# A decode block on one core: the last fourteenth of w2 moved to GpSimd's DMA queue

## The chip, the cores and the metric

The kernel runs on one core of a Trainium2 chip. The core has five engines that run beside each other: TensorE (PE), VectorE (DVE), ScalarE (ACT), GpSimd (POOL) and SyncE (SP). Loads from HBM to SBUF are issued by one of them and carried out by sixteen load engines. The metric is the time of one execution on the device, in microseconds (us). A time quoted as a result is the median of several runs; the profile shows one further execution.

## The reference, cut to what matters

The output is the sum of the input `x`, grouped-query attention over a cache, and a dense layer with Mish, both on the layer-normalised `x`. There are 8 batches with one query each, D = 512, 32 query heads over 8 key heads, 8192 cached positions of 128 values, and F = 1792 hidden values.

```python
xn = _layernorm(x, axis=-1)
return x + _A_ref(xn, A_k_cache, A_v_cache, A_wq, A_wo) + _B_ref(xn, B_w1, B_b1, B_w2)

# _A_ref
q = (x @ wq).reshape(B, Sq, Hq, Dh).transpose(0, 2, 1, 3)
scores = jnp.einsum("bhqd,bhkd->bhqk", q, k) * (Dh ** -0.5)
o = jnp.einsum("bhqk,bhkd->bhqd", _softmax(scores), v)
return o.transpose(0, 2, 1, 3).reshape(B, Sq, Hq * Dh) @ wo

# _B_ref
h = jnp.einsum("bsd,df->bsf", x, w1) + b1
return jnp.einsum("bsf,fd->bsd", mish(h), w2)
```

All data are float32. The caches are nearly all of the 561 MB that each execution reads.

## The kernel before, in words

**Loop.** The work is cut into sixteen packs of two batches and two key heads. For each pack and each of its two batches, 8 MB of keys (`kT`) and 8 MB of values (`v`) come into two big buffers, `kva` and `kvb`. PE forms the scores into the PSUM banks `c0` and `c1` (`scores`), gathers them into `s` (`rows`), DVE and ACT form the weights `pt`, and PE sums the values into `o0` and `o1` (`values`). DVE folds these into `os` (`gather`), PE sums over partitions into `m` (`merge`), and DVE scales them into `oT` (`collect`). At the end of four packs `turn` and `outputs` multiply by a part of `wo`. The Mish half runs once at the start (`mish`); its result, transposed, stays in `aT` until the end of the kernel.

**Order.** A small recording layer (`Program`) keeps the operations of each engine in the order of the code and works out which semaphores each must wait for. An engine runs its operations in that order, so whatever stands behind a waiting operation waits too. All large loads are issued by SP on one queue, in the order of the list `queue`; a load is issued when its buffer is free (`release`, `pump`). Since every recorded operation is issued by one helper, the profile gives nearly all of them the same line (L383), and they are told apart by the names of their tiles.

**End.** After the last pack the code writes out: the sum of the values of the first batch (`values(0)`, from `kvb`), the sums of the weights (`sums`, `over`), two rounds of products whose result nobody reads (`unread(2)`, on `sc` and `ones`, into `c`), `merge(0)`, then `add_up`, which starts the last accumulation in `h` from the four groups of rows of `acc` (`acc` holds `x` and the earlier parts of `wo`), `unread(2)` again, the values of the second batch from `kva` (two loads, `va` with three quarters and `vb` with the last), `gather(1)`, `merge(1)`, `collect(1)`, `turn`. Then come the products of `w2` (`down`) and of the last part of `wo` (`last_outputs`) in five pieces, as they land: 8 of 14 rows of w2, three quarters of wo, 5 rows, the last quarter of wo, 1 row. A "row" of w2 is a block of 128 partitions by 512 columns (256 KB). DVE copies `h` out and SP stores it.

The five pieces go into `kvb`, whose first half is free once `values(0)` has read it; SP waits for a signal of that (`read`), and issues them behind the two loads of the second batch's values.

A product with weights of 8 or 32 columns fills a quarter of PE's columns; four such products to different rows of a bank run beside each other. In the profile, one float32 product is two records.

Of the kernel before, what the change touches and what calls it, by code (L numbers as in the profile page):

```python
# [1 line left out]

# [10 lines left out]
P = 128  # L13
B = 8
D = 512
# [7 lines left out]
G = 4  # L23
# [8 lines left out]
Q = P // G  # L32
# [27 lines left out]
W2R = G * FT // 2 * FP // P  # L60
# [4 lines left out]
LOOPED = ("tensor", "vector", "scalar")  # L65
FIRST, END = 1, PACKS
RARE = ("w",)
SOMETIMES = {
    "turn": lambda p: (p + 27) & 19,
    "queries": lambda p: (p + 1) & 19,  # L70
# [39 lines left out]
class Program:  # L110
# [43 lines left out]

    @staticmethod
    def region(ap):
        (step, n), *free = ap.ap
        p, f = divmod(ap.offset, step)
        return p, p + n, f, f + 1 + sum(s * (c - 1) for s, c in free)

    def conflicts(self, op):

# [281 lines left out]
def kernel(  # L444
# [13 lines left out]
    prog = Program(nc)  # L458
    pe, dve, act, pool, sp = (getattr(prog, e) for e in ("tensor", "vector", "scalar", "gpsimd", "sync"))

    def tile_of(shape, name):
        prog.on_chip.add(name)
        return nc.alloc_sbuf_tensor(name, list(shape), F32).ap()
# [8 lines left out]
    acc = tile_of([P, D], "acc")  # L472
    qc = tile_of([P, B, KR, REP], "qc")
    aT = tile_of([P, 2 * W2R, Q], "aT")
# [8 lines left out]
    def rows_of(blocks):  # L483

        return blocks.rearrange("j p f -> (j p f)").rearrange("(p f) -> p f", p=P)
# [13 lines left out]
    def release(what, relay=None):  # L499

        at = next(at for at, w in taken.items() if w == what)
        del taken[at]
        if relay:
            held[at] = [relay]
        pump()
# [57 lines left out]
    plan_v(PACKS - 1, 0, "b", "v0", lo=KX * BW)  # L563
    plan_v(PACKS - 1, 1, "a", "va", (0, 3 / 4))
    plan_v(PACKS - 1, 1, "a", "vb", (3 / 4, 1))
    W2_PARTS = ((0, 8), (8, 13), (13, 14))
    WO_PARTS = ((0, 3), (3, 4))
    for k, (lo, hi) in enumerate(W2_PARTS):
        plan("w2", "b", w2, ("w2a", "w2b", "w2c")[k], (lo / (2 * W2R), hi / (2 * W2R)))
# [7 lines left out]
    H = bank([P, 512], "h")  # L577
# [42 lines left out]
    os = [tile_of([P, DH], f"os{b}") for b in range(PB)]  # L620
    oT = tile_of([P, 2, REP, B], "oT")
    oW = tile_of([P, OR, 2, B], "oW")

    def setup():
        pool.memset(ident, 0.0)
        pool.affine_select(
            out=ident,
            in_=ident,
            compare_op=ALU.not_equal,
            fill=1.0,  # L630
            base=0,
            pattern=[[-1, P]],
            channel_multiplier=1,
        )
        pool.memset(ones, 1.0)
        dve.memset(xnT, 0.0)
        dve.memset(O[1], 0.0)
        dve.memset(os[1], 0.0)
        dve.memset(rt, 0.0)
        dve.memset(M[:, 168 : 168 + PB * 2 * REP], 0.0)  # L640

        st = tile_of([B, 8], "st")

        scratch = pt.rearrange("p b c m t e h -> p (b c m t e h)")
        xc, sq = scratch[:B, :D], scratch[:B, D : 2 * D]
        dve.reduce_sum(st[:, 0:1], x_sb, axis=AX.X)
        dve.tensor_scalar_mul(st[:, 1:2], st[:, 0:1], 1.0 / D)
        dve.tensor_scalar(xc, x_sb, st[:, 1:2], None, op0=ALU.subtract)
        dve.tensor_mul(sq, xc, xc)
        dve.reduce_sum(st[:, 2:3], sq, axis=AX.X)  # L650
        dve.tensor_scalar(
            st[:, 3:4], st[:, 2:3], 1.0 / D, EPS, op0=ALU.mult, op1=ALU.add
        )
        act.activation(st[:, 4:5], st[:, 3:4], AF.Sqrt)
        dve.reciprocal(st[:, 5:6], st[:, 4:5])

        dve.tensor_mul(st[:, 6:7], st[:, 5:6], st[:, 5:6])
        dve.tensor_mul(st[:, 7:8], st[:, 6:7], st[:, 3:4])
        dve.tensor_scalar(st[:, 6:7], st[:, 7:8], -0.5, 1.5, op0=ALU.mult, op1=ALU.add)
        dve.tensor_mul(st[:, 4:5], st[:, 6:7], st[:, 5:6])  # L660
        dve.tensor_scalar(xc, xc, st[:, 4:5], None, op0=ALU.mult)
        xr = wide[:B, : QR * P]
        pool.tensor_copy(
            xr.rearrange("b (r i s) -> b r i s", r=QR, i=PAIRS),
            xc.rearrange("b (o s r) -> b r o s", o=1, r=QR).to_broadcast([B, QR, PAIRS, P // PAIRS]),
        )
        for r in range(QR):
            pe.transpose(M[:, r * B : (r + 1) * B], xr[:, r * P : (r + 1) * P], ident[:B, :B])
        for i in range(PAIRS):
            rows = slice(Q * i, Q * (i + 1))  # L670
            act.copy(
                xnT[rows, :, :, B * i : B * (i + 1)],
                M[rows, : QR * B]
                .rearrange("p (r o b) -> p r o b", r=QR, o=1)
                .to_broadcast([Q, QR, 2, B]),
            )

        xs = scratch[:B, 2 * D : 2 * D + W1R * P]
        for t in range(2):
            pool.tensor_copy(  # L680
                xs.rearrange("b (r c t i) -> b r c t i", r=W1R, c=CC, t=2)[:, :, :, t, :],
                xc.rearrange("b (c i r) -> b r c i", c=CC, r=W1R),
            )

        dve.tensor_copy(
            gsel, ident[:G, :G].rearrange("p (g o) -> p g o", o=1).to_broadcast([G, G, B])
        )
        dve.reduce_sum(bsel, ident.rearrange("p (u i) -> p u i", u=KN), axis=AX.X)
        dve.reduce_sum(
            half, ident.rearrange("p (g t i) -> p t g i", g=G, t=2), axis=AX.XY  # L690
        )
        dve.reduce_sum(rsel, ident.rearrange("p (g r) -> p r g", g=G), axis=AX.X)
        dve.reduce_sum(hsel, rsel.rearrange("p (i r) -> p r i", i=W4), axis=AX.X)
        dve.reduce_sum(isel, rsel.rearrange("p (i r) -> p i r", i=W4), axis=AX.X)
        dve.tensor_scalar(far, isel, FAR, -FAR, op0=ALU.mult, op1=ALU.add)
        of_head = tile_of([P, 2, V8], "of_head")
        dve.reduce_sum(
            of_head, ident.rearrange("p (e j r) -> p e r j", e=2, j=NB), axis=AX.X
        )
        dve.tensor_copy(tsel, of_head.rearrange("p e (b h) -> p b e h", b=PB))  # L700
        dve.memset(csel, 0.0)
        for c in range(2):
            rows = slice(HE * c, HE * (c + 1))
            for b in range(PB):
                dve.tensor_copy(
                    csel[rows, b, :, b], ident[rows, rows].rearrange("p (u h) -> p u h", u=KN)
                )
        return xs
# [152 lines left out]
    def sums():  # L861
        pe.matmul(M[:, 136 : 136 + PB * 2 * REP], ones, lsel, start=True, stop=True)
# [6 lines left out]
    def values(b, vt, lo=0, hi=ROUNDS):  # L869

        for k in range(lo, hi):
            for c in range(G):
                j = G * k + c
                last = pe.matmul(
                    O[b][Q * c : Q * (c + 1), :],
                    pt[:, b, j % 2, j // 2].rearrange("p t e h -> p (t e h)"),
                    vt[:, W4 * DH * j : W4 * DH * (j + 1)],
                    start=(k == 0),
                    stop=(k == ROUNDS - 1),
                )  # L880
        return last

    def gather(b):

        dve.tensor_scalar(os[b], O[b][:, :DH], isel[:, 0:1], None, op0=ALU.mult)
        for i in range(1, W4):
            dve.scalar_tensor_tensor(
                os[b],
                O[b][:, DH * i : DH * (i + 1)],
                isel[:, i : i + 1],  # L890
                os[b],
                op0=ALU.mult,
                op1=ALU.add,
            )

    def unread(rounds):

        for _ in range(rounds):
            for c in range(G):
                pe.matmul(C[0][Q * c : Q * (c + 1), :], ones[:, :Q], sc, start=True, stop=True)  # L900

    def merge(b):

        at = 168 + b * 2 * REP
        pe.matmul(M[:, at : at + 2 * REP], os[b], hsel, start=True, stop=True)
# [41 lines left out]
    def outputs(w):  # L947
# [12 lines left out]
        dve.tensor_add(acc, H, acc)  # L960
        return read

    def add_up():

        for g in range(G):
            pe.matmul(
                H[Q * g : Q * g + B, :P],
                rsel[:, :B],
                acc[:, g * P : (g + 1) * P],
                start=True,  # L970
                stop=False,
            )
# [70 lines left out]
    def down(lo, hi, w):  # L1043

        for j in range(lo, hi):
            for g in range(G):
                at = j * D + g * P
                pe.matmul(
                    H[Q * g : Q * g + B, :P],
                    aT[:, j, :B],  # L1050
                    w[:, at : at + P],
                    start=False,
                    stop=(j == 2 * W2R - 1),
                )


# [64 lines left out]
    turning()  # L1121
    last = values(0, landed["v", p, 0])
    read = prog.relay("vector", "sync", last)
    gather(0)
    release(("v", p, 0), read)
    sums()
    over()
    unread(2)
    merge(0)
    add_up()  # L1130
    unread(2)
    values(1, landed["v", p, 1], 0, ROUNDS * 3 // 4)
    values(1, landed["v", p, 1], ROUNDS * 3 // 4)
    unread(2)
    gather(1)
# [58 lines left out]
```

## Time and profile before

| what | value |
|---|---|
| median of 3 runs | 1300.78 us (1300.77 to 1300.98) |
| the profiled execution | 1300.95 us, of which its span 1299.6 us |
| read from HBM | 561.01 MB, 432 GB/s over the span |
| PE | 868.1 us busy (67%), 4826 records |
| DVE | 392.7 us busy (30%) |
| ACT | 123.7 us busy (10%) |
| POOL | 8.4 us busy (1%), 11 records |
| SP's queue q1 | 11088 packets, 561.06 MB |
| ACT's queue q10 (x and b1) | 24 packets, 0.02 MB |

The page has one row for each group of like instructions: engine, operation, written tile <- read tiles, shapes, count, busy time. The timeline lists instructions from their start, with the idle time before them and what ended it in brackets. A row with "DMA_DIRECT2D" is the issue of a load; when it lands stands in the table of issues. The table of windows gives for each stretch of time the busy time of PE, PE's weight loads, DVE, ACT and POOL, then the granted clock of PE, the share of the load engines' time that was used, and GB/s. No view tells the sixteen load engines apart.

### The profile page before, as it was taken

How to read it: one execution, taken by the hardware profiler on the slowest of the kernel's cores; microseconds unless marked ns; L12 is line 12 of the kernel's file. 1: busy time of each engine (PE TensorE's matmuls, PEld its weight loads, DVE VectorE, ACT ScalarE, POOL GpSimd, SP SyncE). 2: the span in 40 equal slices, each digit the busy share in tenths (PEclk: the TensorE clock that was granted, in tenths of full speed). 3: DMA queues.
4: the chain of work that ended last, by engine and by line, in shares of the span. 5: the costliest groups of instructions: out<-in, count | busy, mean ns of one | idle time of the engine just before them, and what ended most of it. 6: DMA issues, size and time to landing. Idle time of an engine off the chain costs nothing.

```text
span 1299.6 us, 11355 instructions
## 1 busy us (share of the span) xinstructions
PE 868.1 (67%) x4826; PEld 279.5 (22%) x4826; DVE 392.7 (30%) x597; ACT 123.7 (10%) x298; POOL 8.4 (1%) x11
## 2 busy tenths in 40 slices
PE   3885775665676656875656776566765667756658
PEld 1221221211222112221211222112221221212113
DVE  3623321525023060340505123052320514115061
ACT  1011200102010010200102010020100102001020
POOL 2000000000000000000000000000000000000000
PEclk9898987778988878887888978778888788877789
DMA  9999999999999999999999999999999999999998
GB/s 404 449 420 446 428 440 428 426 444 428 444 428 442 428 440 430 436 432 428 444 428 444 428 440 430 440 430 434 434 428 444 428 442 430 438 432 440 430 425 374
DMA packets 11122, 561.22 MB, mean 432 GB/s; under 512 B 1244, under 2 KB 1376, under 8 KB 1640
## 3 DMA queue, kind: packets, MB, share of 16 engines
q1 hardware_dynamic: 11088, 561.06, 99.7%
q8 instruction: 7, 0.11, 0.0%
q10 hardware_dynamic: 24, 0.02, 0.0%
q14 instruction: 3, 0.02, 0.0%
HBM read 561.01 MB, written 0.07 MB: 432 GB/s over the span
## 4 chain that ended last, share of the span: by engine, by line
DMA 63%; PE 33%; DVE 3%; issue 1%; ACT 0%; SPq 0%; DVEq 0%
DMA kvb<-in_kT 56%; PE c L383 29%; DMA kva<-in_v 5%; PE o L383 3%; DMA kvb<-in_w 1%; DVE raw L383 1%; DVE pt L383 1%; PE m L383 0%; DVE os L383 0%; PE s L383 0%; ACT wide L383 0%; PE h L383 0%; SPq L383 0%; DVE wide L383 0%; DVE nm L383 0%
## 5 line engine op out<-in xcount | busy, mean ns | idle before, releaser
L383 PE MATMUL c<-kvb,qT 128*64 128x512 f32 x1984 | 499.4, 667 | 330.7 <-DMA kvb<-in_kT 309.7
L383 PEld LDWEIGHTS c<-kvb,qT 128*64 128x64 f32 x1984 | 161.2, 154 | 669.0 <-issue 457.5
L383 PE MATMUL o<-kva,pt 128*32 128x512 f32 x1984 | 238.3, 636 | 17.5 <-DMA kva<-in_v 17.0
L383 DVE TENSOR_REDUCE nm<-s 128x1 f32<-128x1024 f32 x16 | 19.6, 1225 | 437.5 <-PE s L383 437.5
L383 DVE STREAM_TRANSPOSE raw<-wide 128x2048 f32<-128x2048 f32 x36 | 125.4, 3483 | 19.5 <-ACT wide L383 17.7
L383 ACT COPY sc<-c 128x512 f32<-128x512 f32 x32 | 18.8, 586 | 959.0 <-PE c L383 959.0
L383 PEld LDWEIGHTS o<-kva,pt 128*32 128x32 f32 x1984 | 64.7, 116 | 182.1 <-issue 148.4
L383 ACT ACTIVATE wide<-s,nms 128x512 f32<-128x512 f32 x128 | 88.0, 688 | 130.4 <-DVE nms L383 66.9
L383 DVE TENSOR_TENSOR oT<-m,rt 128x16 f32 (+1 forms) x17 | 3.0, 175 | 230.6 <-PE m L383 230.6
L383 DVE TENSOR_SCALAR os<-o,isel 128x128 f32<-128x128 f32 x32 | 11.2, 350 | 146.5 <-PE o L383 146.5
L383 DVE TENSOR_TENSOR pt<-raw 64x256 f32<-64x256 f32 x128 | 53.6, 418 | 1.9
L383 DVE TENSOR_TENSOR qT<-qc,bsel 128x1024 f32<-128x1024 f32 x34 | 40.2, 1222 | 9.8 <-PE s L383 9.7
L383 PE MATMUL s<-sc,csel 64*128 64x512 f32 x128 | 36.1, 641 | 8.5 <-ACT sc L383 7.1
L383 DVE TENSOR_TENSOR raw<-raw 128x1024 f32<-128x1024 f32 x32 | 39.2, 1225 | 2.9 <-DVE raw L383 0.2
L383 DVE SCALAR_TENSOR_TENSOR os<-o,isel,os 128x128 f32<-128x128 f32 x96 | 33.7, 351 | 3.4
L383 ACT ACTIVATION_READ_ACCUMULATOR wide<-s,nms 128x1 f32 x128 | 24.7, 193 | 0.0
L383 PE MATMUL m<-hsel,os 128*128 128x8 f32 x66 | 12.7, 265 | 11.9 <-DVE lsel L383 11.9
L383 PE MATMUL m<-ident,nm 128*1 128x128 f32 x16 | 4.3, 270 | 21.6 <-DVE nm L383 21.6
L383 PE MATMUL h<-kva,raw 128*64 128x512 f32 x64 | 15.5, 646 | 4.7 <-DMA kva<-in_wq 4.7
L383 PEld LDWEIGHTS m<-hsel,os 128*128 128x128 f32 x66 | 10.1, 193 | 26.7 <-DVE lsel L383 12.9
L383 PE MATMUL c<-kva,qT 128*64 128x512 f32 x64 | 14.0, 594 | 1.5 <-DMA kva<-in_kT 1.5
L383 PEld LDWEIGHTS s<-sc,csel 64*128 64x128 f32 x128 | 9.6, 184 | 12.9 <-ACT sc L383 12.7
(96 smaller groups left out, 173.6 us busy)
## 6 DMA issues: line engine op xcount, KB each, us to landing
kva<-in_v SPq DMA_DIRECT2D x2, 4096.0 KB, 23.2
kvb<-in_wo SPq DMA_DIRECT2D x3, 2048.0 KB, 29.9
kva<-in_v SPq DMA_DIRECT2D x1, 6144.0 KB, 24.5
kvb<-in_w SPq DMA_DIRECT2D x1, 3584.0 KB, 30.1
kva<-in_v SPq DMA_DIRECT2D x1, 2048.0 KB, 29.1
kvb<-in_w SPq DMA_DIRECT2D x1, 2048.0 KB, 12.5
kvb<-in_wo SPq DMA_DIRECT2D x1, 1536.0 KB, 15.7
kvb<-in_w SPq DMA_DIRECT2D x1, 1280.0 KB, 18.3
```

What stands on the lines that cost most here:

```text
L383: got = getattr(engine, o.method)(*args, **kw)
```

## The change

The fourteenth row of w2 leaves SP's queue. GpSimd issues it as a load of its own (stream `w2x`) once `values(0)` has read `kvb`. It doesn't go to 128 partitions as 512 columns, but to 8 partitions (44, 48, ..., 72) as 16 slots of 512 columns, right behind the other thirteen rows' columns. A three-row load of a piece of `x` (`few`, 3 engines) goes ahead on the same queue, long before; with it the eight engines that carry the 256 KB are to be those numbered 3 to 10.

Since the row now lies on 8 partitions, its hidden values must lie there too: GpSimd spreads the fourteenth column block of `aT` over 16 slots (`spread`) and builds a selector (`pick`) in the tile `qk`, which nobody needs any more; PE multiplies the two into `c1` (`rows_away`), and ACT copies that to `aX`. Then sixteen products of 8 columns of `aX` with 512 columns of `kvb` go into `h`, and DVE adds `h` to `acc` (`down_away`). `add_up` moves behind three quarters of the second batch's values, since it needs that `acc`. The pieces of w2 at the end become 7, 5 and 1 rows. Two clears of the setup move from DVE to GpSimd, and `region`, which the recording layer uses to find overlaps, learns to read the new load's shape.

```diff
+SKIP, TAKE = 3, 8
+FAR_ROW = 44
+SLOTS = P // TAKE
...
-    W2_PARTS = ((0, 8), (8, 13), (13, 14))
+    W2_PARTS = ((0, 7), (7, 12), (12, 13))
...
+    few = tile_of([SKIP, 2 * B], "few")
+    pick, spread, aX = (qk[:, i * P : (i + 1) * P] for i in range(3))
...
-        dve.memset(xnT, 0.0)
+        pool.memset(xnT, 0.0)
...
-        dve.memset(csel, 0.0)
+        pool.memset(csel, 0.0)
...
+    def rest_of_w2(free):
+
+        first = pool.dma_start(
+            few.rearrange("p (t f) -> p t f", t=2),
+            x[:SKIP, : 4 * B].rearrange("p (t f) -> p t f", t=2)[:, :, :B],
+            stream="few",
+            to="gpsimd",
+        )
+        n = 2 * W2R
+        rows = rows_of(w2)[:, (n - 1) * D :].rearrange("(s i) f -> i s f", s=SLOTS)
+        b = place["b"]
+        step = b.ap[0][0]
+        at = bass.AP(
+            tensor=b.tensor,
+            offset=b.offset + FAR_ROW * step + n * D,
+            ap=[[4 * step, TAKE], [D, SLOTS], [1, D]],
+        )
+        pool.dma_start(at, rows, stream="w2x", to="tensor", after=[free])
+        pool.memset(pick, 0.0)
+        pool.tensor_copy(
+            pick[:, FAR_ROW : FAR_ROW + Q].rearrange("p (i c) -> p i c", c=4)[:, :, 0], hsel
+        )
+        pool.tensor_mul(
+            spread.rearrange("p (s b) -> p s b", s=SLOTS),
+            aT[:, 2 * W2R - 1 :, :B].to_broadcast([P, SLOTS, B]),
+            bsel.rearrange("p (s o) -> p s o", o=1).to_broadcast([P, SLOTS, B]),
+        )
+        prog.add(Op("gpsimd", "settle"), [first])
+
+    def rows_away():
+
+        pe.matmul(C[1][:, :P], pick, spread, start=True, stop=True)
+        act.copy(aX, C[1][:, :P])
+
+    def down_away(w):
+
+        for s in range(SLOTS):
+            at = (2 * W2R + s) * D
+            g = s % G
+            pe.matmul(
+                H[Q * g : Q * g + B, :],
+                aX[:, s * B : (s + 1) * B],
+                w[:, at : at + D],
+                start=(s < G),
+                stop=(s >= SLOTS - G),
+            )
+        dve.tensor_add(acc, H, acc)
...
-                    stop=(j == 2 * W2R - 1),
+                    stop=(j == 2 * W2R - 2),
...
     read = prog.relay("vector", "sync", last)
+    free = prog.relay("vector", "gpsimd", last)
     gather(0)
     release(("v", p, 0), read)
+    rest_of_w2(free)
     sums()
     over()
     unread(2)
     merge(0)
+    rows_away()
+    unread(2)
+    down_away(place["b"])
+    values(1, landed["v", p, 1], 0, ROUNDS * 3 // 4)
     add_up()
-    unread(2)
-    values(1, landed["v", p, 1], 0, ROUNDS * 3 // 4)
     values(1, landed["v", p, 1], ROUNDS * 3 // 4)
     unread(2)
```

On PE, between the products of `values(0)` and the end of `values(1)`, stood this before. A row gives the line, the operation, written tile <- read tiles, the shape written and the count; in brackets the semaphores waited for, by stream or engine (`va_tensor` is the landing of the load `va`).

```order
L383 MATMUL m<-lsel,ones 128x16 [waits vector_tensor]
L383 MATMUL c<-sc,ones 32x512 x8
L383 MATMUL m<-hsel,os 128x8 [waits vector_tensor]
L383 MATMUL h<-acc,rsel 8x128 x4
L383 MATMUL c<-sc,ones 32x512 x8
L383 MATMUL o<-kva,pt 32x512 [waits va_tensor]
L383 MATMUL o<-kva,pt 32x512 x23
L383 MATMUL o<-kva,pt 32x512 [waits vb_tensor]
L383 MATMUL o<-kva,pt 32x512 x7
```

At the same place stands now (the helper's line has become L388):

```order
L388 MATMUL m<-hsel,os 128x8 [waits vector_tensor]
L388 MATMUL c<-qk 128x128 [waits gpsimd_tensor]
L388 MATMUL c<-sc,ones 32x512 x8
L388 MATMUL h<-kvb,qk 8x512 [waits scalar_tensor,w2x_tensor]
L388 MATMUL h<-kvb,qk 8x512 x15
L388 MATMUL o<-kva,pt 32x512 [waits va_tensor]
L388 MATMUL o<-kva,pt 32x512 x23
L388 MATMUL h<-acc,rsel 8x128 [waits vector_tensor]
L388 MATMUL h<-acc,rsel 8x128 x3
L388 MATMUL o<-kva,pt 32x512 [waits vb_tensor]
L388 MATMUL o<-kva,pt 32x512 x7
```

One 128x128 product that waits for GpSimd and sixteen products that wait for ACT and for the load `w2x` have come in ahead of the sums on `kva`, and `add_up` (h<-acc,rsel) has moved down.

On GpSimd, the end of its program was this before; the last two rows are the clear of `pt` in the setup and the end of the kernel.

```order
L383 MEMSET ones 128x128
L383 COPY wide<-pt 8x2048 [waits vector_gpsimd]
L383 COPY pt<-pt 8x32x16
L383 COPY pt<-pt 8x32x16 [waits gpsimd_gpsimd]
L383 MEMSET pt 128x2048 [waits vector_gpsimd]
L439 ISA [waits tensor_gpsimd,SP_sequencer_49]
```

Now the two clears (`raw` holds `xnT`) stand in the setup, and behind it the two loads and the three operations on `qk`:

```order
L388 MEMSET ones 128x128
L388 MEMSET raw 128x1024
L388 COPY wide<-pt 8x2048 [waits vector_gpsimd]
L388 COPY pt<-pt 8x32x16
L388 COPY pt<-pt 8x32x16 [waits gpsimd_gpsimd]
L388 MEMSET csel 128x256
L388 MEMSET pt 128x2048 [waits vector_gpsimd]
L388 DMA few<-in_x 3x2x8 [waits tensor_gpsimd]
L388 DMA kvb<-in_w 8x16x512 [waits vector_gpsimd]
L388 MEMSET qk 128x128
L388 COPY qk<-hsel 128x8 [waits gpsimd_gpsimd]
L388 TENSOR_TENSOR qk<-aT,bsel 128x128
```

The three operations on `qk` stand behind the load `w2x` (kvb<-in_w), which waits for DVE's signal that `kvb` is free; the 128x128 product on PE waits for the last of them.

More of the change, by code (lines that the diff above doesn't have):

```diff
@@ L1 @@
+import math
 from contextlib import ExitStack
@@ L156, in region @@
     def region(ap):
-        (step, n), *free = ap.ap
-        p, f = divmod(ap.offset, step)
-        return p, p + n, f, f + 1 + sum(s * (c - 1) for s, c in free)
+        row = math.prod(ap.tensor.shape[1:])
+        p, f = divmod(ap.offset, row)
+        down = sum(s // row * (n - 1) for s, n in ap.ap if s >= row)
+        return p, p + down + 1, f, f + 1 + sum(s * (n - 1) for s, n in ap.ap if s < row)
     def conflicts(self, op):
```

## The prediction

> **What bounds the kernel now.** I read the page's line of DMA share and its queue table first, then the end of the chain of waits, then PE's timeline of the last 24 us, then the transfers' landings and the DMA share in short windows at the end.
>
> ```profile
> DMA  9999999999999999999999999999999999999998
> q1 hardware_dynamic: 11088, 561.06, 99.7%
> ...
> 1266.15 9.88 PE o L383 x64
> ...
> 1276.95 18.31 DMA kvb<-in_w
> ...
> 1297.70 0.29 DVE acc L383
> ```
>
> SP's queue q1 keeps the sixteen load engines busy in every fortieth of the span. So the bytes set the time, and the change alters none of them: what can move is the end. There the chain hangs on a load of w2, not on an engine.
>
> ```profile
> 1276.23 1.93 PE L383 MATMUL c<-sc,ones 128*32 128x512 f32 x16
> 1278.08 0.39 PE L383 MATMUL m<-hsel,os 128*128 128x8 f32 x2
> 1278.40 0.41 PE L383 MATMUL h<-acc,rsel 128*8 128x128 f32 x8
> 1278.62 1.90 PE L383 MATMUL c<-sc,ones 128*32 128x512 f32 x16
> 1280.34 7.05 PE L383 MATMUL o<-kva,pt 128*32 128x512 f32 x64
> ...
> 1290.73 1.93 PE L383 MATMUL h<-kvb,aT 128*8 128x128 f32 x64
> 1292.48 1.49 PE L383 MATMUL h<-kvb,oW 128*8 128x128 f32 x48
> 1295.31 1.28 PE L383 MATMUL h<-kvb,aT 128*8 128x128 f32 x40 [1.34 <-DMA kvb<-in_w]
> 1296.59 0.62 PE L383 MATMUL h<-kvb,oW 128*8 128x128 f32 x16
> 1297.23 0.40 PE L383 MATMUL h<-kvb,aT 128*8 128x128 f32 x8
> ```
>
> PE works without a pause from 1276 until it reaches the last loads. How long would it have been ready earlier? Go from start to start: 64 records of 128 columns take 1292.48 - 1290.73 = 1.75 us, 0.0273 us each. The 48 of wo need 1.31 and would hand over at 1293.79, but the next start is 1295.31: a wait of 1.52. The 40 need 1.09, to 1296.40, next start 1296.59: 0.19. The 16 need 0.44, to 1297.03, next start 1297.23: 0.20. **PE's slack against the loads is 1.52 + 0.19 + 0.20 = 1.91 us.**
>
> ```profile
> kvb<-in_w SPq DMA_DIRECT2D x1, 256.0 KB, 19.3
> ...
> 1294.50:1295.10 0.60, 0.00 (x0) 0.00 (x0) 0.00 (x0) 0.00 (x0) 0.00 (x0) 1.00 1.01 393
> 1295.10:1295.50 0.40, 0.19 (x8) 0.19 (x12) 0.00 (x0) 0.00 (x0) 0.00 (x0) 1.00 0.73 292
> 1295.50:1295.90 0.40, 0.40 (x24) 0.40 (x20) 0.00 (x0) 0.00 (x0) 0.00 (x0) 1.00 0.54 195
> 1295.90:1296.30 0.40, 0.40 (x25) 0.40 (x16) 0.00 (x0) 0.00 (x0) 0.00 (x0) 1.00 0.44 154
> 1296.30:1296.70 0.40, 0.39 (x16) 0.11 (x8) 0.00 (x0) 0.00 (x0) 0.00 (x0) 1.00 0.21 77
> ...
> 1277.90 0.43 SPq L383 DMA_DIRECT2D kvb<-in_w  x1
> 1298.02 0.35 SPq L383 DMA_DIRECT2D out<-acc  x1
> ...
> out<-acc SPq DMA_DIRECT2D x1, 64.0 KB, 1.6
> ```
>
> The last 256 KB of w2, issued at 1277.90, land 19.3 us later, 1297.2, where PE's last eight records start. The windows' last but one column, the DMA share, falls from 1.01 to 0.73, 0.54, 0.44, 0.21: some engines are done 1.5 us before the others. The views name no engine.
>
> **The change part by part.** *Loads.* The 256 KB were 16 KB on each of sixteen engines; now 32 KB on eight. At 27.2 GB/s an engine (435 GB/s in the row below, over 16) 16 KB is 0.60 us: engines without a share end 0.60 earlier, those with one 0.60 later. If engines 3 to 10 are the early ones, the loads end 0.6 us sooner, at 1296.6; if not, up to 0.6 later. That is all that can be won.
>
> *PE.* Ahead of the sums on kva stand sixteen new products, 8 columns of weights by 512 of kvb, plus one of 128x128.
>
> ```profile
> L383 PE MATMUL h<-kvb,oW x48: 592/761/1061, 458.5 to 1088.1; 128*8 128x512 f32 x48
> ...
> 1280.30:1287.20 6.90, 6.90 (x68) 2.08 (x64) 0.00 (x0) 0.00 (x0) 0.00 (x0) 1.00 1.02 435
> ```
>
> Products of just that shape (8 by 512, h<-kvb,oW) last at best 592 ns a record, as the page's c<-sc ones of 32 by 512 do, so I give them the same pace: 16 records from 1278.62 to 1280.34, 1.72 us. Sixteen products are 32 records: **+3.44**. The 128x128 product is two records with full weights, like m<-hsel,os, 1278.08 to 1278.40: **+0.32**. The moved add_up costs the same at its new place. The row that leaves takes 8 records of 128 columns off the end: **-0.22**. Slack: **-1.91**. Sum **+1.63 us** with no new wait. The extra sum on DVE reads h while PE is in the next 5 us of values, so that hides it.
>
> *New waits.* PE's 128x128 product waits for GpSimd, the sixteen wait for the 256 KB; behind either, the whole rest of PE stands. With no wait the sixteen begin at 1278.40 + 0.32 + 1.72 = 1280.44.
>
> ```profile
> 2.34 0.20 POOL L383 MEMSET ident<- 128x128 f32 x1 [1.90 <-SPq L1150]
> ...
> 13.52 2.31 POOL L383 COPY pt<-pt 8x512 f32<-8x512 f32 x2
> 18.27 1.80 POOL L383 MEMSET pt<- 128x2048 f32 x1 [2.45 <-DVEq L380]
> ...
> 1276.10 0.33 SPq L383 DMA_DIRECT2D kvb<-in_w  x1
> ```
>
> GpSimd hears of the free buffer when SP does, 1276.1. It issues the load (not in this trace: between SP's 0.33 and, taking the 2.31 us of its slowest pair of copies, 2.3; I take 1.0, nearer SP's row), clears 128 columns (0.20), copies 8, multiplies 128 (0.5, estimated from the copy's 1.15 us for 512). That is ready at 1278.0, or 1279.3 if the issue takes 2.3; PE gets there at 1278.40, so I take nothing (bounds 0 and 0.9).
>
> The 256 KB: a hardware load on idle engines takes 1.6 us to land (out<-acc); 32 KB an engine instead of 4 KB adds 1.0; of the rows of kva ahead in q1 (2,048 KB over 128 partitions, 16 KB and 0.60 us each) two go first, as two did before b1 (next fence), and one more before the completion word: 1.8; an issue of 1.0 instead of 0.33 adds 0.7. 1276.1 + 1.6 + 1.0 + 1.8 + 0.7 = 1281.2. Bounds: 1279.4 with nothing ahead, and the first rival's 1289. I take 1281.2, since it goes by the nearest rows for start, turn and pace: the sixteen start 0.76 late. **Sum: +1.63 + 0.76 = +2.4 us.**
>
> The trace shows how two queues share an engine: b1 comes by ACT's queue beside the first rows of wq, and I counted its packets in four windows (2.5 to 7.3, 7.3 to 7.6, 7.6 to 9.8, 9.8 to 10.0 us).
>
> ```profile
> 1.37 0.26 ACTq L383 DMA_DIRECT2D acc<-in_b  x1
> ...
> q1 hardware_dynamic: 17, 1.11, 53.5%
> ...
> q10 hardware_dynamic: 4, 0.01, 6.2%
> ...
> q1 hardware_dynamic: 6, 0.39, 41.2%
> ...
> q10 hardware_dynamic: 4, 0.00, 1.1%
> ```
>
> Issued at 1.4, its four rows (q10) move only at 7.3 to 7.6, and its four completion words only at 9.8 to 10.0, one 64 KB row (2.4 us at 27 GB/s) later. So a hardware queue gets one row a turn. Whether the software queue gives up its turn after each 2 KB row no row here shows; it decides everything. [...]
>
> *Setup.* Two clears go from DVE to GpSimd; 128x1024 is half of the 1.80 us row. PE then waits for wq anyway, 4.68 us:
>
> ```profile
> 22.83 15.48 PE L383 MATMUL h<-kva,raw 128*64 128x512 f32 x64 [4.68 <-DMA kva<-in_wq]
> ```
>
> Nothing, then, and behind it stands a queue full of loads. The three-row load of x moves some hundred bytes in mid-stream: nothing.
>
> **The rivals.** *Row by row* (0.26). The 2 KB rows take turns with q1's rows as b1's did: from about 1278.5, five turns behind kva's 16 KB (0.68 each with its own row), eight behind w2's 14 KB (0.61), four behind wo's 12 KB (0.53): 10.4 us, landing near 1289. PE stands 8.4 us: +1.63 + 8.4 = +10.0. A pause also costs pace:
>
> ```profile
> 1265.56 0.59 PE L383 MATMUL m<-hsel,os 128*128 128x8 f32 x2 [11.94 <-DVE lsel L383]
> ```
>
> behind this idle time of 11.94 us the 64 records of values took 9.88 us (chain, above) against 7.05 at 1280.34, so up to 2.8 more here. About 1312, bounds 1311 to 1314. *Two rows a turn* (0.12): nine turns, landing near 1285, +1.63 + 4.4, and up to 1.5 for pace: about 1307.
>
> *DVE in GpSimd's way* (0.06). DVE works right where GpSimd issues:
>
> ```profile
> 1276.55 1.12 DVE L383 SCALAR_TENSOR_TENSOR os<-o,isel,os 128x128 f32<-128x128 f32 x3
> 1277.60 0.25 DVE L383 RECIPROCAL rt<-m 128x16 f32<-128x16 f32 x1
> ```
>
> If the issue stood until 1277.85, the load would land 1.75 later: +4.4, 1305.3. [...]
>
> *The loads still decide* (0.06), the other side. If the sixteen products cost PE under 1.5 us (their weights fill 8 columns), PE stays ahead of loads ending 0.6 us sooner: 1300.3, no slower. The point is a shift of PE of 1.91 + 0.22 - 0.6 = 1.5; the 592 ns rows speak against it. *Other engines than 3 to 10* (0.05): the loads end up to 0.6 us later, still before PE, which then ends 2.4 us later: as forecast.
>
> **How the numbers follow.** The profiled execution took 1300.95 us (span 1299.6 and 1.35 around it), 0.17 over the median of 1300.78. 1300.95 + 2.4 = **1303.4**, the likeliest (0.45, bounds 1302.6 to 1304.8, as GpSimd and the landing move it). The range reaches up into the row-by-row case and leaves out its end and the case with the loads: 1302.3 to 1313. About 0.2%, 2.6 us, can be told from no change; the forecast sits at that edge, half of it on either side. Slower: 0.45 x 0.5 + 0.26 + 0.12 + 0.06 + half of 0.05 = 0.69, taken as 0.66, for terms that may each be a few tenths smaller; same 0.32; faster 0.02, as no term gives over 0.6 us.
>
> **What would show it.** The sixteen h<-kvb,qk start at 1280.4 to 1282 (1285 or 1289 for the turn-takers) and take 3.4 us; the last records of h follow each other without a wait for kvb<-in_w, and the chain's end names PE's o and h in place of the 18.31 us of DMA. A software queue whose packets lie together for some 1.3 us bears out the sum; spread over ten us, the rival. If PE still waits for w2 at the end, the slack or the price of the sixteen was wrong.

## The result, and the profile after

| kernel | median, us | lowest to highest |
|---|---|---|
| before | 1300.88 | 1300.75 to 1300.98 (6 runs) |
| after | 1310.49 | 1309.31 to 1311.59 (6 runs) |

The ratio is 1.0074, with a 95% interval of 1.0064 to 1.0085: the change costs 9.6 us. The execution profiled after it took 1311.59 us, with a span of 1310.1; against the profiled execution of before that is 10.6 us more, of which the span has 10.5. All lines of the recording layer are now L388.

The page of the kernel after, its DMA share in forty slices and its queues (packets, MB, share of the engines' time):

```profile
DMA  9999999999999999999999999999999999999995
...
q1 hardware_dynamic: 11088, 560.80, 98.9%
q0 software_dynamic: 176, 0.26, 0.1%
```

The last slice has fallen from 8 to 5. The load engines are done and something else goes on. The end of the chain of waits of the kernel after (start, us, what) says what it is:

```profile
1276.52 9.80 DMA kvb<-in_w
1286.33 0.04 issue
1286.37 6.54 PE h L388 x32
1292.91 5.15 PE o L388 x48
...
1303.41 4.75 PE h L388 x168
1308.15 0.02 issue
1308.18 0.29 DVE acc L388
```

Before, 18.31 us of DMA stood in the chain, with only the last 2.4 us of PE's products between them and the last copy. Now the chain goes through the 256 KB that GpSimd issues, then through the sixteen products, and from there PE sets the end. The timeline of the same execution:

```profile
1276.52 0.63 POOL L388 DMA_DIRECT2D kvb<-in_w  x1 [1229.60 <-DVEq L385]
1276.69 1.12 DVE L388 SCALAR_TENSOR_TENSOR os<-o,isel,os 128x128 f32<-128x128 f32 x3
...
1277.59 0.40 POOL L388 TENSOR_TENSOR qk<-aT,bsel 128x128 f32<-128x128 f32 x1
...
1278.11 0.39 PE L388 MATMUL m<-hsel,os 128*128 128x8 f32 x2
...
1278.35 0.47 PE L388 MATMUL c<-qk 128*128 128x128 f32 x2
...
1278.75 1.92 PE L388 MATMUL c<-sc,ones 128*32 128x512 f32 x16
...
1286.37 6.54 PE L388 MATMUL h<-kvb,qk 128*8 128x512 f32 x32 [5.70 <-DMA kvb<-in_w]
...
1292.74 5.32 PE L388 MATMUL o<-kva,pt 128*32 128x512 f32 x48
```

GpSimd is ready at 1277.99 and PE gets to the 128x128 product at 1278.35, so that is no wait. The unread rounds take 1.72 and the sixteen could start at 1278.75 + 1.72 = 1280.47; they start at 1286.37, **5.90 late**. From their start to the next they take 6.37 us instead of 3.44, **2.93 more**. The table of windows (PE, its weight loads, DVE, ACT, POOL, granted clock, DMA share, GB/s) shows the clock:

```profile
1280.40:1286.40 6.00, 0.30 (x8) 0.03 (x8) 0.00 (x0) 0.00 (x0) 0.00 (x0) 0.92 1.02 433
1286.40:1292.70 6.30, 6.30 (x32) 1.17 (x36) 0.00 (x0) 0.00 (x0) 0.00 (x0) 0.53 0.99 416
1292.70:1297.90 5.20, 5.20 (x55) 1.43 (x50) 0.69 (x1) 0.00 (x0) 0.00 (x0) 1.00 0.62 256
```

While the sixteen run, the granted clock is 0.53; in the work behind them it is 1.00. That the pause brought this on is shown by experiment 3 below. DVE's extra sum (0.69) lies beside PE's next work, as forecast. The DMA share of the last window is 0.62: the loads end in it, while PE still has ten microseconds to go.

The shift adds up. The start of the sums on kva moves from 1280.34 to 1292.74, 12.40 = 0.13 (the 128x128 product in, add_up out) + 5.90 + 6.37. Behind it PE needs 15.44 us to the last copy (1308.18) where it needed 17.36 (1280.34 to 1297.70): 1.92 less, its waits for the loads (1.91) and eight records (0.22) gone and add_up (0.22) there. 12.40 - 1.92 = 10.48, the 10.5 by which the span grew.

The table of issues of after (KB, us from issue to landing), GpSimd's load and the last one of SP:

```profile
kvb<-in_w POOLq DMA_DIRECT2D x1, 256.0 KB, 9.8
kvb<-in_w SPq DMA_DIRECT2D x1, 256.0 KB, 19.9
```

SP's last piece, issued at 1277.92, lands near 1297.8, later than the 1297.2 of before and not sooner. For GpSimd's load I counted packets in four windows, 1276.5 to 1280.3 (none of q0), and then 1280.3 to 1281.0, 1281.0 to 1285.4 and 1285.4 to 1286.1:

```profile
DMA packets 33, 0.31 MB, mean 445 GB/s; under 512 B 8, under 2 KB 8, under 8 KB 16
...
q0 software_dynamic: 16, 0.03, 12.0%
...
DMA packets 245, 1.86 MB, mean 422 GB/s; under 512 B 80, under 2 KB 80, under 8 KB 136
...
q0 software_dynamic: 120, 0.23, 13.5%
...
q0 software_dynamic: 8, 0.00, 0.6%
```

Packets between 2 and 8 KB number 8 in the first of these and 136 - 80 = 56 in the second: 64 for the 256 KB, so **each is 4 KB, two of the 2 KB slots**, eight to each of the eight engines that are to carry it. None moves in the first 3.2 us after the issue ended (1277.15). Then the eight of an engine are spread over five microseconds, at 13% of the engines' time, with rows of q1 between.

### The profile page after: what moved, and what is told of

Its sections match the earlier page's. It is cut to its first block, busy times and chain, and to the rows that moved or that the text cites. A ratio compares the mean times of both kernels' runs of the same rounds, so it can differ in the third digit from the quotient of the medians.

```text
span 1310.1 us, 11417 instructions
## 1 busy us (share of the span) xinstructions
PE 873.2 (67%) x4852; PEld 281.2 (21%) x4852; DVE 392.0 (30%) x596; ACT 123.9 (9%) x299; POOL 11.7 (1%) x18
## 4 chain that ended last, share of the span: by engine, by line
DMA 60%; PE 35%; DVE 4%; issue 1%; ACT 0%; SPq 0%; DVEq 0%
DMA kvb<-in_kT 51%; PE c L388 29%; DMA kva<-in_v 8%; PE o L388 5%; DVE raw L388 2%; DVE pt L388 1%; PE h L388 1%; DMA kvb<-in_w 1%; PE m L388 1%; DVE os L388 0%; PE s L388 0%; ACT wide L388 0%; DVE wide L388 0%; DVE nm L388 0%; DVE lsel L388 0%
## 5 line engine op out<-in xcount | busy, mean ns | idle before, releaser
L388 PE MATMUL c<-kvb,qT 128*64 128x512 f32 x1984 | 503.4, 672 | 333.4 <-DMA kvb<-in_kT 301.8
L388 PEld LDWEIGHTS c<-kvb,qT 128*64 128x64 f32 x1984 | 162.6, 155 | 674.1 <-issue 437.8
L388 PE MATMUL o<-kva,pt 128*32 128x512 f32 x1984 | 233.3, 624 | 16.2 <-DMA kva<-in_v 15.7
L388 DVE TENSOR_REDUCE nm<-s 128x1 f32<-128x1024 f32 x16 | 19.6, 1225 | 442.1 <-PE s L388 442.1
L388 DVE STREAM_TRANSPOSE raw<-wide 128x2048 f32<-128x2048 f32 x36 | 125.7, 3492 | 19.5 <-ACT wide L388 17.7
L388 ACT COPY sc<-c 128x512 f32<-128x512 f32 x32 | 18.8, 586 | 958.8 <-PE c L388 958.8
L388 PEld LDWEIGHTS o<-kva,pt 128*32 128x32 f32 x1984 | 63.6, 114 | 176.6 <-issue 144.1
L388 ACT ACTIVATE wide<-s,nms 128x512 f32<-128x512 f32 x128 | 88.0, 688 | 130.6 <-DVE nms L388 66.9
L388 DVE TENSOR_TENSOR oT<-m,rt 128x16 f32 (+1 forms) x17 | 3.0, 176 | 229.5 <-PE m L388 229.5
L388 DVE TENSOR_TENSOR pt<-raw 64x256 f32<-64x256 f32 x128 | 53.5, 418 | 1.9
L388 DVE TENSOR_SCALAR os<-o,isel 128x128 f32<-128x128 f32 x32 | 11.2, 349 | 139.9 <-PE o L388 139.9
L388 DVE TENSOR_TENSOR qT<-qc,bsel 128x1024 f32<-128x1024 f32 x34 | 40.2, 1222 | 9.8 <-PE s L388 9.8
L388 PE MATMUL s<-sc,csel 64*128 64x512 f32 x128 | 36.1, 641 | 8.5 <-ACT sc L388 7.1
L388 DVE TENSOR_TENSOR raw<-raw 128x1024 f32<-128x1024 f32 x32 | 39.2, 1225 | 2.9 <-DVE raw L388 0.2
L388 DVE SCALAR_TENSOR_TENSOR os<-o,isel,os 128x128 f32<-128x128 f32 x96 | 33.7, 351 | 3.4
L388 ACT ACTIVATION_READ_ACCUMULATOR wide<-s,nms 128x1 f32 x128 | 24.7, 193 | 0.0
L388 PE MATMUL m<-hsel,os 128*128 128x8 f32 x66 | 12.7, 265 | 11.9 <-DVE lsel L388 11.9
L388 PE MATMUL h<-kva,raw 128*64 128x512 f32 x64 | 15.6, 648 | 5.1 <-DMA kva<-in_wq 5.1
L388 PE MATMUL m<-ident,nm 128*1 128x128 f32 x16 | 4.3, 270 | 21.6 <-DVE nm L388 21.6
L388 PEld LDWEIGHTS m<-hsel,os 128*128 128x128 f32 x66 | 10.1, 193 | 26.7 <-DVE lsel L388 12.8
L388 PE MATMUL c<-kva,qT 128*64 128x512 f32 x64 | 14.0, 594 | 1.4 <-DMA kva<-in_kT 1.4
L388 PEld LDWEIGHTS s<-sc,csel 64*128 64x128 f32 x128 | 9.6, 184 | 12.9 <-ACT sc L388 12.7
```

Source lines behind the costliest of these rows:

```text
L388: got = getattr(engine, o.method)(*args, **kw)
```

## The experiments

Each was timed beside the kernel before, whose median was 1300.8 to 1301.0 each time. Intervals are of the ratio to it. `T` is the theory read off above: late first packet, 4 KB a turn, then half clock.

**1. The sixteen behind the last values.** Nothing then waits for the 256 KB.

```diff
     unread(2)
-    down_away(place["b"])
     values(1, landed["v", p, 1], 0, ROUNDS * 3 // 4)
-    add_up()
     values(1, landed["v", p, 1], ROUNDS * 3 // 4)
-    unread(2)
+    down_away(place["b"])
```

The sum on DVE (`acc`) and `add_up` follow behind `collect` and `turn`.

> The sixteen products, add_up and the sum on DVE stand behind both parts of the second batch's values, in place of the two unread rounds there. Theory T (the 256 KB of GpSimd's queue go in turns with q1's 16 KB rows, land at 1286.3, and PE stands in front of them): the data are there when PE arrives at 1287.4, no wait for w2x, and PE is late by only about 1.9 us of its 2.1 us slack, so the end waits for the last piece of w2 again: 1301.5 us (1300.5 to 1302.6). Rival W (the added work on PE, or the disturbance of q1 by the second queue, is the cost): the work is still on PE's path and the second queue still runs, 1306 us or more.

Measured: 1301.73 us, ratio 1.0007 (0.9997 to 1.0016). PE's timeline:

```profile
1286.59 3.62 PE L388 MATMUL h<-kvb,qk 128*8 128x512 f32 x32
...
1295.83 1.28 PE L388 MATMUL h<-kvb,aT 128*8 128x128 f32 x40 [0.76 <-DMA kvb<-in_w]
...
1297.94 0.61 PE L388 MATMUL h<-kvb,aT 128*8 128x128 f32 x8 [0.27 <-DMA kvb<-in_w]
```

Without the wait the same load and the same products cost 8.8 us less (the two unread rounds that are gone lie where PE waits for the loads anyway). The sixteen run at full pace (3.62 in the row, as in experiment 2) and the end hangs on the loads again.

**2. The sixteen on other data.** They stay where the change put them and read `kva`, which is there.

```diff
-            at = (2 * W2R + s) * D
+            at = s * D
...
-    down_away(place["b"])
+    down_away(place["a"])
```

GpSimd waits for the load at its end. The result isn't the reference's: it holds products with the values in place of the fourteenth row.

> The sixteen products read the values in kva, which have landed at 1278.9, and so don't wait for the 256 KB; those are loaded as before but read by nobody, so the fourteenth row of w2 is missing from the result. Theory T: the sixteen start at 1280.4 and take 3.4 us, PE ends 1.6 us late: 1302.5 us (1301.8 to 1303.3). Rival W: the sixteen themselves are slow (6.5 us as in the changed kernel), 1305.5 us or more.

Measured: 1302.68 us, ratio 1.0013 (1.0003 to 1.0022). PE's timeline:

```profile
1279.01 3.62 PE L388 MATMUL h<-kva,qk 128*8 128x512 f32 x32
1282.44 5.33 PE L388 MATMUL o<-kva,pt 128*32 128x512 f32 x48
...
1298.37 0.50 PE L388 MATMUL h<-kvb,oW 128*8 128x128 f32 x10 [1.00 <-issue]
```

1282.44 - 1279.01 = 3.43: the price of the products was right. The sum without a wait, 1300.95 + 1.63 = 1302.58, agrees too, but in the execution profiled this is luck in part. Near its end PE stands 1.00 us for nothing that the profile shows (last row above). And PE came to this stage 1.45 us earlier than in the profile of before; here is the first product behind `values(0)`, before and then in this experiment:

```profile
1275.90 0.40 PE L383 MATMUL m<-lsel,ones 128*128 128x16 f32 x2
...
1274.45 0.40 PE L388 MATMUL m<-lsel,ones 128*128 128x16 f32 x2
```

The two nearly cancel: from the sums on kva to the last copy PE needs 16.79 us here (1282.44 to 1299.23) where it needed 15.44 in the change, 1.35 more. The same product starts at 1274.25 to 1275.93 in the profiles of all twelve kernels, so the slack of 1.91 us is the figure of one execution.

**3. PE kept busy up to the landing.**

```diff
     rows_away()
-    unread(2)
+    unread(9)
     down_away(place["b"])
```

> Nine unread rounds instead of two between the 128x128 product and the sixteen, about as long as the wait. Theory T with its second part (the sixteen ran at half pace because PE had stood still for 5.7 us): the sixteen start at 1286.5 as before but take 3.4 us instead of 6.4, so 7.6 us over the kernel before, 1308.4 us (1307.6 to 1309.2). Rival (half pace is the price of products with 8 columns on this data, or of loads writing kvb at the time): the sixteen take 6.4 us again, 1311 us or more.

Measured: 1308.77 us, ratio 1.006 (1.0043 to 1.0077), 1.7 us less than the change itself; the spans of the two profiled executions, 1307.6 and 1310.1, are 2.5 apart. PE's timeline:

```profile
1286.82 3.62 PE L388 MATMUL h<-kvb,qk 128*8 128x512 f32 x32 [1.32 <-DMA kvb<-in_w]
1290.26 5.33 PE L388 MATMUL o<-kva,pt 128*32 128x512 f32 x48
```

The sixteen wait until 1286.8, about as in the change, and take 3.44; the granted clock of the window 1286.40 to 1292.70 is 1.00, where the change had 0.53. So the half clock came of PE's standing, not of the data or of the loads beside it.

**4. ACT's hardware queue** issues the same load.

```diff
-        pool.dma_start(at, rows, stream="w2x", to="tensor", after=[free])
+        act.dma_start(at, rows, stream="w2x", to="tensor", after=[near])
...
+    near = prog.relay("vector", "scalar", last)
```

`near` is DVE's signal that `kvb` is free, sent to ACT; GpSimd's first operation on `qk` now waits for `free`.

> As the changed kernel, but the 256 KB are issued by ACT on its hardware queue at the same point (2 KB rows, sixteen on each of eight engines). Theory T (one packet a turn, and a hardware queue's packet is one 2 KB row where the software queue's was two): twice as many turns, landing near 1289 (12 to 13 us after the issue), the sixteen start 8.5 us late and run at half pace, 1313 us (1311 to 1315). [...]

Measured: 1315.55 us, ratio 1.0112 (1.0096 to 1.0129). Its page's q10 has 160 packets, 136 more than before: 128 rows of 2 KB and 8 words. The timeline has the issue and the products:

```profile
1275.80 0.81 ACTq L388 DMA_DIRECT2D kvb<-in_w  x1
...
1291.29 5.38 PE L388 MATMUL h<-kvb,qk 128*8 128x512 f32 x32 [11.14 <-DMA kvb<-in_w]
1296.50 5.32 PE L388 MATMUL o<-kva,pt 128*32 128x512 f32 x48
```

Sixteen turns of 2 KB where GpSimd's queue took eight of 4 KB: PE starts 15.5 us after the issue instead of 9.9. This is the first rival's mechanism, on the other queue: the load is slow there too. The time lies past the range expected, since the 12 to 13 us from issue to landing were too few: over 3 us pass before the first packet, and the turns behind it take over ten. ACT's issue ended at 1276.61, the window 1276.6 to 1279.7 has no packet of q10, and the window 1279.7 to 1280.4 has the first:

```profile
q10 hardware_dynamic: 7, 0.01, 5.2%
```

That is the same 3 us as on GpSimd's queue, so the delay doesn't come of GpSimd's part in the issue.

**5. Fewer, longer rows:** the same 256 KB as eight rows of 32 KB (another piece of w2, so that part of the result isn't the reference's).

```diff
-        rows = rows_of(w2)[:, (n - 1) * D :].rearrange("(s i) f -> i s f", s=SLOTS)
+        flat = w2.rearrange("j p f -> (j p f)")
+        rows = flat[F * D - P * D :].rearrange("(i f) -> i f", i=TAKE)
...
-            ap=[[4 * step, TAKE], [D, SLOTS], [1, D]],
+            ap=[[4 * step, TAKE], [1, SLOTS * D]],
```

> The same 256 KB to the same eight partitions, but read from eight stretches of 32 KB in HBM (the last 256 KB of the array), so that each engine has one row instead of sixteen; the fourteenth row of w2 is not what lands, so that part of the result is wrong. Theory T: one turn instead of eight, first byte at 1280.4 as before, 1.2 us of transfer, a turn before the completion word: landing at 1282.6, PE stands 2.2 us, 1304.7 us (1303.5 to 1306.5). Rival (the software queue is late by itself, whatever the rows): landing at 1286 and 1310 us as before.

Measured: 1307.78 us, ratio 1.0059 (1.0043 to 1.0076): earlier, but 3 us past what was expected. The table of issues (KB, us to landing):

```profile
kvb<-in_w POOLq DMA_DIRECT2D x1, 256.0 KB, 7.7
```

PE's timeline:

```profile
1283.25 5.32 PE L388 MATMUL h<-kvb,qk 128*8 128x512 f32 x32 [3.58 <-DMA kvb<-in_w]
1288.39 5.33 PE L388 MATMUL o<-kva,pt 128*32 128x512 f32 x48
```

And GpSimd's queue in the window 1279 to 1280, where the issue was at 1275.52:

```profile
q0 software_dynamic: 16, 0.26, 97.5%
```

All eight rows start in this one microsecond and take 0.975 x 16 / 8 = 1.95 us each, where 32 KB at 27.2 GB/s is 1.2. The first packet comes as late as in the change. And 3.58 us of standing was already enough to slow the sixteen, to 5.14. Both were missing in the expectation.

**6. Shorter rows in q1:** the last quarter of the values (`vb`) comes as four loads with 4 KB rows, so that each turn of q1 is short.

```diff
-    plan_v(PACKS - 1, 1, "a", "vb", (3 / 4, 1))
+    for i in range(12, 16):
+        plan_v(PACKS - 1, 1, "a", f"vb{i}", (i / 16, (i + 1) / 16))
```

> As the changed kernel, but the last quarter of the second batch's values (vb) is issued by SP as four loads with rows of 4 KB instead of one with rows of 16 KB; the 256 KB on GpSimd's queue keep their eight packets an engine. Theory T (the price is the length of q1's rows in the turns between): a turn is 0.16 + 0.16 us instead of 0.6 + 0.16, eight of them 2.6 us, landing near 1283 (6.5 us after the issue instead of 9.8), PE stands about 2.5 us and the sixteen are slowed in part, 1306 us (1304 to 1307.5). Rival (GpSimd's queue delivers at its own pace, or the eight packets wait for something else than q1): landing near 1286 and 1310 us as in the changed kernel.

Measured: 1304.98 us, ratio 1.0034 (1.0021 to 1.0046). The table of issues:

```profile
kvb<-in_w POOLq DMA_DIRECT2D x1, 256.0 KB, 6.8
```

PE's timeline:

```profile
1282.25 3.62 PE L388 MATMUL h<-kvb,qk 128*8 128x512 f32 x32 [2.72 <-DMA kvb<-in_w]
```

What lies between the turns set the landing here: 6.8 us from the issue instead of 9.8, with the load itself untouched. (In experiments 1 to 3 and 7 to 9, whose loads are those of the change or differ in the set of engines alone, it is 10.9 to 11.6.) After 2.72 us of standing the sixteen run at full pace, where the expectation had them slowed in part.

Experiment 2 is the change without a wait. The kernels of this table differ from it by the time that PE stands and by what the sixteen take over 3.44, and these two make up the measured times to within 0.9 us:

| kernel | PE stood, us | sixteen took, us | 1302.68 + both | median, us |
|---|---|---|---|---|
| shorter rows in q1 | 2.72 | 3.44 | 1305.4 | 1304.98 |
| rows of 32 KB | 3.58 | 5.14 | 1308.0 | 1307.78 |
| the change | 5.70 | 6.37 | 1311.3 | 1310.49 (1311.59 as profiled) |
| ACT's queue | 11.14 | 5.21 | 1315.6 | 1315.55 |

The loss of pace doesn't grow with the stand: 1.70 us after 3.58, 2.93 after 5.70, 1.77 after 11.14. Windows laid along the granted clock show what it follows; the first is the change, the next two the rows of 32 KB, the last ACT's queue:

```profile
1285.48:1292.31 6.83, 5.94 (x29) 1.07 (x33) 0.00 (x0) 0.00 (x0) 0.00 (x0) 0.50 1.00 424
...
1283.25:1284.05 0.80, 0.80 (x8) 0.23 (x12) 0.00 (x0) 0.00 (x0) 0.00 (x0) 1.00 1.03 440
1284.05:1287.46 3.41, 3.41 (x20) 0.71 (x16) 0.00 (x0) 0.00 (x0) 0.00 (x0) 0.50 0.99 420
...
1291.29:1294.90 3.61, 3.61 (x20) 0.73 (x24) 0.00 (x0) 0.00 (x0) 0.00 (x0) 0.50 0.98 376
```

The clock stands at 0.50 for a stretch, and the sixteen lose half of what they spend in it: half of 5.94, 3.41 and 3.61. With rows of 32 KB it fell only 0.80 us after PE had begun again. So in these three runs the price was set by where the stretch lies, and not by how long PE stood.

**7. The load alone,** without its products: what does it do to the end of the loads?

```diff
-    rows_away()
+    add_up()
     unread(2)
-    down_away(place["b"])
     values(1, landed["v", p, 1], 0, ROUNDS * 3 // 4)
-    add_up()
```

GpSimd waits for the load at its end.

> The 256 KB are loaded by GpSimd's queue as in the change and read by nobody; the 128x128 product, the sixteen and the sum on DVE are left out and add_up stands where it did before, so the fourteenth row of w2 is missing from the result. What the load side alone is worth: if engines 3 to 10 were the early ones, the last piece of w2 lands 0.6 us sooner and it takes 1300.2 us; by the landings of the changed kernel (its last piece came at 1297.9, 0.7 later than before) some of the eight are late ones, and it takes 1301.5 us (1301.0 to 1302.0).

Measured: 1301.71 us, ratio 1.0007 (0.9997 to 1.0016). The interval reaches 1, so by the times alone this could be nothing; but the loads don't end sooner.

**8 and 9. Other engines,** in the form of experiment 1:

```diff
-SKIP, TAKE = 3, 8
-FAR_ROW = 44
+SKIP, TAKE = 5, 8
+FAR_ROW = 52
```

and in another kernel `SKIP, TAKE = 1, 8` with `FAR_ROW = 36`.

> The version with the sixteen behind the values, but five rows in the small load ahead instead of three and the eight partitions moved with it (52, 56, ... 80), so that the eight engines are the next two further on. If the load side sets the end, the time follows the set of engines: 1300.3 us if all eight are early ones, 1301.7 as with 3 to 10, up to 1302.5 if more late ones are among them. If PE sets it, 1301.7 as before.

> The same with one row in the small load and partitions 36, 40, ... 64: engines two further down. Same expectation: between 1300.3 and 1302.5 us by the set if the loads set the end, and then not the same as the version two further up; 1301.7 if PE sets it.

Measured: 1301.69 us (1.0007, 0.9998 to 1.0017) and 1302.24 us (1.0012, 1.0002 to 1.0022), against 1301.73 for the set meant to be 3 to 10. Which engines a set falls on was the author's assumption; no run shows it. No set is shown to be better than the one chosen, and none wins anything.

**10. All sixteen engines:** as experiment 7, but GpSimd loads the row as before, 512 columns on 128 partitions.

```diff
-        pool.dma_start(at, rows, stream="w2x", to="tensor", after=[free])
+        x2 = pool.dma_start(b[:, (n - 1) * D : n * D], rows_of(w2)[:, (n - 1) * D :], stream="w2x", to="gpsimd", after=[free])
```

> Left out: the sixteen products on the fourteenth row of w2, and with them that row's part of the result. The edit: as in the run that only loaded the 256 KB (it took 1301.71 us), but GpSimd loads the fourteenth row as the kernel before did, 512 columns on each of 128 partitions, so that all sixteen load engines carry 16 KB of it; nobody reads it, and SP's queue ends with the thirteenth row. Theory E, the eight engines: the 0.9 us that the load alone cost came of laying 256 KB on eight engines, some of which were late ones; here the loads end as they did in the kernel before, and since PE has eight records fewer at the end, the time is 1300.6 (1300.3 to 1301.1), and the lags of the last load's completion words among the engines shrink from about 2.8 us to 1.7 or less. Theory Q, the second queue: the software queue itself costs the load engines that time (turns, its descriptors), whichever engines carry it; then 1301.5 to 1302, with lags as wide as in the run that loaded on eight.

Measured: 1301.21 us, ratio 1.0002 (0.9993 to 1.0011), between what the two theories expected. The windows at the end, 1294.50 to 1295.10, then 1296.70 to 1297.10, of experiment 7:

```profile
1294.50:1295.10 0.60, 0.00 (x0) 0.00 (x0) 0.00 (x0) 0.00 (x0) 0.00 (x0) 1.00 0.80 314
...
1296.70:1297.10 0.40, 0.39 (x16) 0.28 (x16) 0.00 (x0) 0.00 (x0) 0.00 (x0) 1.00 0.11 41
```

and of experiment 10:

```profile
1294.50:1295.10 0.60, 0.00 (x0) 0.00 (x0) 0.00 (x0) 0.00 (x0) 0.00 (x0) 1.00 0.99 386
...
1296.70:1297.10 0.40, 0.38 (x16) 0.11 (x8) 0.00 (x0) 0.00 (x0) 0.00 (x0) 1.00 0.00 0
```

With eight engines some stand idle early (0.80) and others still work at the end (0.11); with sixteen all are busy, then all done. The sixteen completion words of the last load say the same: spread over 2.7 us in experiment 7 and 1.6 in experiment 10, 1.7 in the kernel before. The spans go with the theory of the eight engines: their medians are 1299.5 in experiment 10 and 1299.5 to 1299.6 in the kernel before, and 1299.9 in experiment 7. What is left of both times lies outside the span: 1.7 us around it in these two kernels, 1.35 before and 1.33 in experiment 1. In both, GpSimd and not PE waits for the load. But it does so in experiment 2 too, which has 1.46, and in experiment 4, where PE waits, it is 1.67; so the cause stays open.

None of these kernels is faster than the one before.

## Why the prediction was right in its sign and 7 us short

Forecast was 1303.4; the median is 1310.49, inside the range and between the time of two rows a turn (1307) and that of row by row (1312). The likeliest case, with its bounds of 1302.6 to 1304.8, missed; that the range holds the result is owed to the rivals, up to which it was drawn.

- **What bounds the kernel, and the slack of 1.91:** right. The waits for the loads at the end are gone in the kernel after, and 1.92 came off.
- **Sixteen products 3.44, the 128x128 product 0.32, -0.22, sum +1.63 without a wait:** right in its parts: 3.43 and 3.44 for the sixteen in experiments 2 and 3, and 0.35 for the 128x128 product (0.13 with add_up gone from its old place, 0.22 for add_up at the new one). The total agrees with experiment 2 (1302.58 and 1302.68), in part by the luck told there. The 592 ns rows were the right neighbours, and the rival that the loads still decide falls with that.
- **GpSimd ready at 1278.0:** right (1277.99), by two misses that cancel: GpSimd began 0.39 later than SP (1276.52 and 1276.13), and its issue took 0.63 and not 1.0. The issue ended beside DVE's three sums (1276.69 to 1277.81), and ACT's queue, in whose issue GpSimd has no part, had the same delay to its first packet, so DVE in GpSimd's way falls too; that GpSimd's issue stands while DVE works no run shows. (That rival's own terms, 1.63 + 0.76 + 1.75, give 4.1 and 1305.1, not 4.4 and 1305.3.)
- **The landing at 1281.2: this is the step that failed.** That two rows of kva "go first" and "one more before the completion word" supposed that the sixteen rows go in one turn, which no run shows. They went in eight, 4 KB at a time: the mechanism of *two rows a turn*, which had 0.12. That rival put the landing near 1285, since it let the first turn begin at 1278.5; the first packet moved at 1280.3 or later, and the landing was 1286.3. 5.9 us of waiting stood where the sum had 0.76. The turns are not the whole miss: in experiment 5 each engine took its share in one turn, and still the load landed 7.7 us after its issue, where the sum had 5.1 from 1276.1. The sum's 1.6 for a load on idle engines came from the row of the output's store; here the first packet alone took over 3 us from the end of the issue.
- **Pace:** the sum had nothing for it, which would have been right for a wait of 0.76 (stands of 1.32 and 2.72 cost no pace in experiments 3 and 6); the rivals had up to 1.5 and up to 2.8. It was 2.93, the whole of it after half the idle time of the row quoted. Experiment 3 shows that the stand was its cause.
- **Load side, 0.6 either way:** the favourable sign isn't borne out. In the change it is hidden, since PE sets the end; the load alone has 0.4 us more of span and 0.9 more of time, with an interval that reaches 1.

The row of b1 spoke truly of a hardware queue: experiment 4 has one 2 KB row a turn. It said nothing of the software queue, and the text said so; the step between them was a choice. The trace of before had one stand to price others by, 11.94 us with up to 2.8 us of pace. The runs have more of them: 1.32 and 2.72 us of standing left the pace alone (experiments 3 and 6), 3.58 cost 1.70 (experiment 5), 5.70 cost 2.93 (the change) and 11.14 cost 1.77 (experiment 4). Nothing was run between 2.72 and 3.58.

## What to carry to other kernels

Beside a saturated first queue, the small load on a second one didn't take its own time here but waited at each of its turns for what the first queue had in between: 256 KB landed 9.8 us after the issue, and 6.8 us after it where SP's last quarter of the values came in 4 KB rows. Price such a load as the number of turns (here 4 KB each on GpSimd's queue, one 2 KB row each on ACT's) times the row ahead, plus the delay before its first packet (here some 3 us from the end of the issue). Where PE waited for the load, a long stand cost more than itself, since the next work ran at a granted clock of 0.50 for a while: nothing was added to stands of up to 2.72 us, and 1.7 to 2.9 us to those of 3.58 to 11.14; put the consumer behind work that is long enough, as experiment 1 does (1301.73 us instead of 1310.49). Moving bytes between load engines that no view tells apart is a gamble: three sets of eight gained nothing (0.9 to 1.4 us more, at the edge of what the intervals tell), and sixteen even shares stayed level in the span.

## What the runs showed of the hardware that was not expected

- Some 3 us pass between the end of GpSimd's issue and its first packet (from 1277.15 to 1280.3 or later in the kernel after, from 1276.06 to 1279 or later in experiment 5), though the issue itself takes only 0.54 to 0.63. On ACT's queue it is the same (from 1276.61 to 1279.7 or later, experiment 4). What fills this time no view shows.
- A row of 32 KB took 1.95 us on an engine (experiment 5) where the pace of the loads would give 1.2.
- In experiment 2 PE stood 1.00 us for nothing that the profile shows. The window 1296.0 to 1297.4 just ahead has one packet of the queue q8, listed as "instruction", 16 KB, whose transfer took 4.2% of 16 engines for 1.4 us, 0.94 us. That the one caused the other was not tested; the kernel after has such a packet in the window 1304.5 to 1306.0, and PE doesn't stand there.

```profile
q8 instruction: 1, 0.02, 4.2%
```
